# A fused attention and gMLP block on one core: first loads from two queues, all h tiles transposed by DMA, no centred keys, part of the 1/sigma work on GpSimd, and early idle products on a constant

## The chip, the cores and the metric

The kernel runs on one core of one Trainium2 chip. A core has TensorE (PE, matrix products), VectorE (DVE), ScalarE (ACT), GpSimd (POOL) and SyncE (SP, which here only issues transfers); 16 DMA engines move the data. The metric is the time of one execution on the device in microseconds (us). The kernel before was timed three times: 246.90, 246.95 and 247.34 us, median 246.95 us.

## The reference

One sequence of 2048 tokens with 512 features in bf16 goes through two residual blocks. `ln` is layernorm over the features without gain or offset.

```
h   = x + A(ln(x))
out = h + B(ln(h))

A(u):  q, k, v = split(u @ wqkv)              # 32 heads of 16 features
       phi(t) = (t + 1 if t > 0 else exp(t)) + 1e-6
       kv  = sum over tokens of phi(k) v^T     # 16 x 16 per head
       z   = sum over tokens of phi(k)
       o   = (phi(q) kv) / (phi(q) . z + 1e-6)
       return o @ wo
B(u):  z   = gelu(u @ w_in)                    # 512 -> 1792
       z1, z2 = halves of z, 896 features each
       g   = w_sp @ ln(z2) + b_sp              # w_sp: 2048 x 2048, mixes the tokens
       return (z1 * g) @ w_out                 # 896 -> 512
```

## The kernel before

All of the data stays in SBUF. The 2048 tokens are 16 tiles of 128 tokens, and four groups of four tiles. Every operation is recorded by `op(engine, cost, ...)` with what it reads and writes; a list `ORDER` (lines 15 to 52) then says in which order the operations go to the five instruction queues, and a list `SLOT` which PSUM bank or buffer each temporary tile gets. Each engine works through its queue strictly in that order, and waits by semaphores are added where an operand comes from another engine. So the order of the work on each engine is written out, and an instruction whose operand is late holds up all that stand behind it on its engine.

The stages, with the lines that matter here:

1. Loads (lines 503 to 513). SP issues x tiles 0, 1, 2-3, then the key weights `wk`, then x tiles 4-5, 6-7, 8-11, 12-15 and the query weights `wq`, in this order. The weights `wv`, `wo`, `w_in` come later from POOL (lines 709 to 711), once the last transpose of x has landed.
2. Idle products (lines 548 to 552). While the first tiles are on their way, PE runs 14 products of 128x512 on a tile of zeros, which VectorE clears first (line 516). They compute nothing that is used.
3. Layernorm of x (lines 619 to 640). For each tile, `stats` (line 557) and `aggr` (line 561) on VectorE give mean and variance; Ln and Exp on ScalarE (`rstd_act`, lines 571 and 573) give 1/sigma, from tile 4 on for two tiles at a time; `normalise` (line 583) on VectorE writes the normalised tile. Then it is transposed (`transposed`, line 598): tiles 2 to 5 by four PE products against an identity (line 612) and a ScalarE copy out of PSUM (line 615), the others by a DMA transpose that SP issues (line 604). Tiles 0 and 1 have a second path (`CENTRED`): the tile less its mean, not yet divided by sigma (line 633), is transposed by PE, and their keys are made from it; 1/sigma comes in as the scale of ScalarE's Exp and Relu on the product (line 649).
4. Keys and queries. `kv_proj` makes the keys of a pair of tiles (line 673), `phi` applies exp (line 652), for some pairs also Relu (line 654), and finishes on VectorE: with a min (line 655) and an add (line 658) where Relu was taken by ScalarE, and with the min and one longer instruction from PSUM (line 661) where it wasn't. PE then adds up x^T phi(k) over all tiles (line 705), from which kv follows later without making v. `q_proj` (line 687) makes the queries transposed, a group of four tiles at a time, and so needs all four transposed tiles of that group.
5. The denominators (`den`: lines 787 to 818), and `h`: the products of line 837, the residual add of line 842, stats and aggr of h, 1/sigma on POOL (`rstd_pool`, lines 576 and 578, and `minus`, lines 593 and 594), `normalise_act` on ScalarE (line 589), and the transpose of the normalised h tile: tiles 0 to 3 by PE and a ScalarE copy, tiles 4 to 15 by DMA. ORDER takes group 1 first, then 2 and 3, and group 0 last.
6. The gMLP: z2 by token tiles (line 869), its gelu (line 874), stats and normalisation; z1 transposed by feature blocks (line 900), which needs a whole group of h; the mixing products with the DMA-transposed `w_sp` (line 939, transposes issued on line 915); the gate on VectorE (946, 948); the last projection (957), residual (963) and store (965).

SP's queue is one row: the loads, the 12 DMA transposes of x, the 16 transposes of the first quarter of w_sp, the 12 of h, the other 48 of w_sp, the stores. POOL's queue holds, among the 1/sigma work of h, the load of `b_sp` (line 927), whose buffer lies over that of phi's temporaries and is free only when the last of these has been read (line 814).

Of the kernel before, what the change touches and what calls it, by code (L numbers as in the profile page):

```python
# [10 lines left out]
P = 128  # L11
# [4 lines left out]
    28, 9, 16, 0, 23, 15, 24, 29, 1, 14, 25, 30, 2, 10, 31, 17, 3, 20, 32, 18, 4, 33, 12, 19, 5, 34, 13, 43, 26, 6,  # L16
    35, 11, 52, 27, 36, 7, 21, 44, 37, 53, 8, 45, 38, 48, 22, 39, 54, 57, 46, 49, 68, 58, 40, 55, 47, 41, 61, 42, 56,
    137, 50, 62, 69, 51, 75, 63, 138, 70, 64, 77, 71, 65, 139, 76, 78, 66, 72, 79, 89, 67, 73, 80, 97, 74, 149, 140,
    81, 84, 82, 141, 119, 150, 83, 99, 85, 142, 120, 158, 87, 86, 143, 151, 88, 159, 144, 59, 145, 152, 160, 60, 90,
    147, 153, 146, 91, 148, 92, 100, 161, 154, 93, 156, 95, 94, 155, 127, 157, 162, 219, 96, 220, 98, 128, 109, 101,  # L20
    102, 117, 164, 221, 166, 103, 110, 167, 118, 104, 129, 222, 107, 168, 121, 130, 223, 122, 131, 251, 108, 224,
    169, 125, 252, 123, 111, 105, 170, 163, 106, 165, 112, 253, 171, 257, 115, 113, 254, 172, 258, 114, 132, 174,
    255, 259, 135, 177, 116, 133, 256, 260, 178, 124, 173, 261, 179, 186, 262, 126, 175, 180, 176, 181, 187, 134,
    183, 188, 185, 136, 182, 189, 196, 605, 197, 190, 191, 205, 606, 198, 215, 184, 206, 607, 199, 217, 200, 193,
    207, 192, 608, 276, 216, 208, 277, 609, 209, 270, 210, 278, 610, 271, 279, 194, 611, 272, 201, 280, 218, 281,
    273, 612, 203, 231, 211, 274, 613, 275, 213, 232, 234, 195, 233, 202, 614, 204, 212, 214, 615, 263, 235, 295,
    264, 616, 282, 265, 236, 283, 617, 266, 284, 237, 296, 267, 269, 618, 238, 239, 297, 241, 242, 268, 289, 298,
    619, 243, 290, 240, 299, 620, 285, 300, 291, 342, 288, 292, 343, 286, 357, 293, 344, 358, 294, 225, 347, 301,
    287, 226, 302, 359, 387, 303, 227, 345, 304, 388, 360, 305, 346, 348, 307, 349, 228, 351, 372, 350, 306, 373,
    352, 361, 362, 353, 402, 229, 355, 354, 363, 230, 364, 417, 366, 374, 365, 418, 356, 367, 389, 368, 403, 370,  # L30
    369, 244, 377, 245, 390, 371, 246, 464, 465, 404, 470, 466, 419, 471, 480, 375, 472, 422, 247, 481, 378, 248,
    250, 577, 482, 467, 578, 423, 249, 574, 579, 405, 621, 575, 391, 483, 376, 325, 392, 381, 576, 379, 484, 380,
    308, 420, 382, 485, 309, 421, 393, 406, 383, 424, 407, 396, 394, 486, 385, 473, 426, 384, 395, 474, 425, 487,
    310, 397, 386, 326, 427, 398, 475, 488, 313, 580, 399, 327, 400, 571, 430, 401, 311, 572, 581, 489, 428, 502,
    330, 573, 503, 328, 496, 312, 490, 504, 331, 314, 408, 512, 491, 315, 329, 468, 317, 316, 505, 497, 409, 332,
    469, 506, 318, 513, 476, 498, 410, 507, 591, 477, 322, 333, 499, 334, 588, 514, 411, 478, 335, 412, 479, 582,
    492, 592, 500, 493, 413, 515, 518, 494, 414, 495, 589, 516, 501, 519, 517, 508, 590, 509, 323, 583, 520, 510,
    585, 511, 415, 521, 528, 324, 416, 522, 584, 523, 438, 524, 525, 336, 429, 439, 527, 337, 586, 440, 526, 431,
    319, 529, 441, 622, 587, 534, 442, 443, 320, 530, 544, 623, 321, 604, 531, 545, 338, 532, 624, 432, 339, 533,
    546, 448, 625, 547, 449, 548, 433, 626, 450, 549, 550, 434, 451, 627, 551, 452, 599, 435, 552, 628, 453, 436,  # L40
    600, 553, 340, 554, 629, 593, 601, 437, 555, 444, 602, 556, 341, 445, 630, 557, 454, 603, 446, 559, 631, 569,
    447, 558, 455, 570, 632, 535, 456, 563, 536, 633, 457, 564, 458, 537, 634, 596, 565, 459, 538, 460, 597, 461,
    539, 635, 540, 560, 541, 598, 463, 462, 636, 561, 543, 542, 670, 562, 637, 671, 672, 673, 638, 674, 675, 566,
    639, 676, 677, 640, 567, 678, 680, 679, 568, 641, 642, 643, 683, 681, 644, 682, 645, 686, 646, 684, 685, 647,
    648, 689, 687, 649, 688, 650, 651, 692, 690, 652, 691, 653, 695, 654, 693, 694, 655, 656, 594, 696, 657, 698,
    697, 595, 658, 659, 701, 660, 699, 700, 661, 662, 704, 702, 663, 703, 664, 665, 707, 705, 706, 666, 667, 710,
# [9 lines left out]
    2, 3, 0, 0, 1, 6, 2, 3, 4, 3, 2, 2, 1, 0, 6, 4, 2, 2, 6, 0, 4, 0, 2, 0, 6, 6, 6, 4, 0, 0, 4, 6, 2, 6, 4, 6, 0, 6,  # L56
    2, 0, 0, 4, 0, 2, 2, 7, 0, 6, 0, 7, 1, 6, 2, 7, 3, 6, 0, 7, 1, 6, 2, 4, 3, 5, 0, 4, 1, 5, 2, 4, 0, 5, 1, 4, 2, 5,
    3, 4, 3, 5, 0, 4, 1, 5, 2, 4, 3, 5, 0, 4, 1, 5, 0, 4, 1, 5, 2, 4, 3, 5, 2, 4, 3, 5, 0, 4, 1, 5, 2, 4, 3, 5, 0, 4,
    1, 5, 2, 4, 3, 5, 0, 4, 1, 5, 2, 4, 3, 5, 0, 4, 1, 5, 2, 4, 3, 2, 0,
]  # L60


# [972 lines left out]
```

## Time and profile before

| what | us |
|---|---|
| median of three runs | 246.95 |
| the profiled execution | 247.78 |
| span of its profile, first to last instruction | 246.0 |
| PE busy | 240.4 |
| VectorE busy | 135.6 |
| ScalarE busy | 89.2 |
| POOL busy | 26.4 |

The span is 1.8 us shorter than the execution that it comes from: what lies around the first and last instruction is not in it. PE is busy for 98% of the span, in products that overlap: a 128x512 product lasts 379 ns by itself, and in a row one starts every 216 ns (96 products of line 939 in 20.72 us). A wait in this profile is idle time of an engine and is put down to what ended it; as ends of products are modelled, a gap in PE's row of products is up to 0.2 us longer than its wait.

### The profile page before, as it was taken

To read this page: it belongs to the slowest core of one execution; us is meant where nothing else is said; L and a number is where in the kernel's file an instruction comes from. 1 tells how busy PE (TensorE), PEld (TensorE's weight loads), DVE (VectorE), ACT (ScalarE), POOL (GpSimd) and SP (SyncE) were. 2 spreads that over 40 slices of the span, in tenths; PEclk is the share of its full clock that TensorE was granted. 3 is DMA by queue.
4 is the path that set the end of the run, shared out by engine and by line. 5 is a ranking of instruction groups with operands and counts; after the bars stand their busy time and mean duration, and the time that the engine had idled before them with its cause. 6 is when DMAs were issued, how large, how long until landed. Compare 5 with 4: busy or idle time off the path is not lost.

```text
span 246.0 us, 3055 instructions
## 1 busy us (share of the span) xinstructions
PE 240.4 (98%) x1189; PEld 109.6 (45%) x1189; DVE 135.6 (55%) x272; ACT 89.2 (36%) x125; POOL 26.4 (11%) x75
## 2 busy tenths in 40 slices
PE   7898999999999999999999999999999999999995
PEld 3443444344334444554444444444444444444443
DVE  5899654579999987585422331352322523323443
ACT  3766946696697777966410010000000000000000
POOL 6000003000503373302300000000000000000000
PEclk9999999999999999999999999999999999999999
DMA  6913358984142301596344444443000110000022
GB/s 199 331 24 68 64 100 248 351 106 94 21 67 85 81 9 31 109 237 95 87 102 98 103 85 101 97 101 109 0 0 0 43 45 0 0 0 3 0 85 85
DMA packets 54494, 21.30 MB, mean 87 GB/s; under 512 B 48368, under 2 KB 53616, under 8 KB 54480
## 3 DMA queue, kind: packets, MB, share of 16 engines
q1 hardware_dynamic: 53536, 16.79, 30.7%
q0 software_dynamic: 944, 4.33, 5.2%
q8 instruction: 9, 0.15, 0.3%
q14 instruction: 5, 0.04, 0.1%
HBM read 7.47 MB, written 2.10 MB: 39 GB/s over the span
## 4 chain that ended last, share of the span: by engine, by line
PE 83%; DVE 6%; ACT 5%; DMA 3%; POOL 1%; issue 0%
PE ps L939 39%; PE ps L957 10%; PE ps L900 10%; PE ps L869 9%; PE ps L673 4%; PE ps L705 4%; PE ps L687 3%; PE ps L550 2%; DMA xT_pq_z<-pk_xn_z 2%; DMA hT<-xn 2%; PE ps L837 1%; DVE small L557 1%; ACT e L649 1%; DVE xh L842 1%; ACT e L652 1%; DVE e L655 1%
## 5 line engine op out<-in xcount | busy, mean ns | idle before, releaser
L939 PE MATMUL ps<-wsp,pk_xn_z 128*128 128x512 bf16 x336 | 73.5, 379 | 0.0
L946 DVE TENSOR_TENSOR e<-ps,e 128x512 bf16<-128x512 f32 x28 | 19.4, 692 | 69.0 <-PE ps L939 69.0
L939 PEld LDWEIGHTS ps<-wsp,pk_xn_z 128*128 128x128 bf16 x336 | 32.9, 98 | 39.6
L869 PE MATMUL ps<-win,hT 128*128 128x384 bf16 (+1 forms) x128 | 26.2, 353 | 0.2 <-DMA hT<-xn 0.2
L900 PE MATMUL ps<-hT,win 128*128 128x512 bf16 x112 | 26.3, 379 | 0.0
L905 ACT ACTIVATE xT_pq_z<-ps 128x1024 bf16<-128x1024 f32 (+1 forms) x16 | 14.6, 915 | 31.6 <-PE ps L900 31.6
L957 PE MATMUL ps<-wout,xT_pq_z 128*128 128x512 bf16 (+1 forms) x119 | 24.7, 366 | 0.0
L939 PE MATMUL ps<-wqkv_wsp,pk_xn_z 128*128 128x512 bf16 x112 | 24.3, 379 | 0.0
L557 DVE BATCH_NORM_STATS2 small<-xh 128x6 f32<-128x512 bf16 x32 | 20.8, 677 | 2.7 <-DMA xh<-in_A_x_dram 2.7
L878 DVE BATCH_NORM_STATS2 small<-pk_xn_z 128x6 f32<-128x512 bf16 (+1 forms) x32 | 18.5, 610 | 4.9 <-ACT pk_xn_z L874 4.9
L652 ACT ACTIVATE e<-ps 128x1024 bf16<-128x1024 f32 x15 | 15.4, 1028 | 6.8 <-PE ps L673 5.6
L869 PEld LDWEIGHTS ps<-win,hT 128*128 128x128 bf16 x128 | 12.2, 98 | 12.6 <-DVE xh L842 0.6
L963 DVE TENSOR_TENSOR e<-ps,xh 128x512 bf16<-128x512 f32 (+1 forms) x17 | 11.2, 660 | 11.3 <-PE ps L957 11.2
L957 PEld LDWEIGHTS ps<-wout,xT_pq_z 128*128 128x128 bf16 x119 | 11.7, 98 | 12.8
L939 PEld LDWEIGHTS ps<-wqkv_wsp,pk_xn_z 128*128 128x128 bf16 x112 | 10.9, 98 | 13.2
L900 PEld LDWEIGHTS ps<-hT,win 128*128 128x128 bf16 x112 | 10.8, 98 | 12.1
L705 PE MATMUL ps<-pk_xn_z 128*128 128x512 bf16 x64 | 15.8, 379 | 0.0
L874 ACT ACTIVATE pk_xn_z<-ps 128x896 bf16<-128x896 f32 x16 | 14.3, 914 | 3.1 <-PE ps L869 3.0
L687 PE MATMUL ps<-xT_pq_z,wqkv_wsp 128*128 128x512 bf16 x64 | 15.3, 380 | 0.0
L673 PE MATMUL ps<-wqkv_wsp,xT_pq_z 128*128 128x512 bf16 x56 | 13.9, 380 | 1.4 <-DMA xT_pq_z<-pk_xn_z 0.8
L837 PE MATMUL ps<-pk_xn_z,xT_pq_z 128*128 128x512 bf16 x64 | 14.8, 379 | 0.2 <-ACT e L812 0.2
L589 ACT ACTIVATE xn<-xh,small 128x512 bf16<-128x512 bf16 x16 | 12.6, 810 | 3.7 <-POOL small L594 3.7
(82 smaller groups left out, 190.6 us busy)
## 6 DMA issues: line engine op xcount, KB each, us to landing
out_dram<-e SPq DMA_DIRECT2D x15, 128.0 KB, 1.7
win<-in_B_w_in_dram POOLq DMA_DIRECT2D x1, 1792.0 KB, 9.1
wqkv_wsp<-in_A_wqkv_dram SPq DMA_DIRECT2D x2, 512.0 KB, 6.1
xh<-in_A_x_dram SPq DMA_DIRECT2D x2, 512.0 KB, 6.6
wout<-in_B_w_out_dram POOLq DMA_DIRECT2D x1, 896.0 KB, 6.6
xh<-in_A_x_dram SPq DMA_DIRECT2D x3, 256.0 KB, 4.9
wsp<-in_B_w_sp_dram SPq DMA_TRANSPOSE x48, 2.9
wqkv_wsp<-in_A_wqkv_dram POOLq DMA_DIRECT2D x1, 512.0 KB, 4.9
```

Source lines behind the costliest of these rows:

```text
L557: op("dve", dve_c(512), lambda e: e.bn_stats(s6.ap(), src.ap()), r=[src], w=[s6])
L652: op("act", act_c(n), lambda e: e.activation(lo.ap(), t(flat).ap(), ACT.Exp), r=[t()], w=[lo])
L673: i = e.matmul(t(bank(ti)).ap(), lhsT=lhs.ap()[:, c, :], rhs=rhs.ap()[:, c, :], start=(c == 0), stop=(c == KD - 1))
L687: r_ = e.matmul(t(bank(i)).ap(), lhsT=lhs.ap()[:, c, :], rhs=rhs.ap()[:, c, :], start=(c == 0), stop=(c == KD - 1))
L705: r = e.matmul(txk[h](bank(i)).ap(), lhsT=xx.ap()[:, c * P:(c + 1) * P], rhs=kk.ap(), start=(n == 0), stop=(n == NT - 1))
L837: i = e.matmul(t(bank(ti)).ap(), lhsT=l.ap()[:, c, :], rhs=mw[c, :].ap(), start=(c == 0), stop=(c == KD - 1))
L869: k = e.matmul(t(bank(i)).ap()[:, 0:b - a], lhsT=l.ap()[:, c, :], rhs=win[c, a:b].ap(), start=(c == 0), stop=(c == KD - 1))
L878: op("dve", dve_c(b - a), lambda e, s6=s6, src=src: e.bn_stats(s6.ap(), src.ap()), r=[src], w=[s6])
L900: k = e.matmul(t(bank(i)).ap(), lhsT=l.ap()[:, c, :], rhs=r_.ap()[:, c, :], start=(c == 0), stop=(c == KD - 1))
L939: k = e.matmul(t(bank(0)).ap(), lhsT=l.ap()[:, s - a, :], rhs=r_.ap()[:, s - a, :], start=(s == 0), stop=(s == NT - 1))
L946: op("dve", dve_c(512), lambda e: e.tensor_tensor(gb().ap(), t(bank(0)).ap(), bsp().ap()[:, tg * GW:(tg + 1) * GW], ALU.add), r=[t(), bsp( ...
L957: k = e.matmul(t(bank(0)).ap()[:, 0:b - a], lhsT=l.ap()[:, fc, :], rhs=wout[fc, a:b].ap(), start=(fc == 0), stop=(fc == KF - 1))
```

## The change

The loads of x tile 1 and of x tiles 2-3 are issued by ScalarE, ahead of its table load; `wk` follows x tile 0 at once in SP's queue. The keys of tiles 0 and 1 are made from the normalised tile as the others are; tiles 0 to 5 are transposed by PE, tiles 6 to 15 by DMA. All 16 tiles of h are transposed by DMA. For tiles 4-5, 6-7, 8-9, 10-11, 12-13 and 14-15 of x, 1/sigma is worked out by POOL (an add and a power) and no longer by ScalarE (Ln and Exp). Relu is taken by ScalarE for key pairs 1, 3, 5 and 7 (before: 0, 3, 5 and 7). The tile of zeros is gone: nine 128x512 idle products and fourteen 128x128 ones read a constant 1.0 that the program always has, with a step of zero. Eleven of the short ones stand right behind the nine, one each between the first three transposes, and the last behind the key product of tile 3.

ORDER and SLOT are new as a whole. What moved in the queues: on PE all four query products of group 0 now stand between key product 4 and the first uses of the keys (line 705); before, two of them stood behind those and two at the end of the h stage; group 0 of h is made first and not last; the z2 tiles go 0 to 8, 10, 13, 11, 14, 15, 12, 9. On VectorE, tile 1's stats come ahead of tile 0's, and tile 0 is normalised behind the stats of tiles 2 and 3. On POOL, `wo` is loaded ahead of `wv` and `w_in`, and `b_sp` is loaded behind the 1/sigma of h tiles 0 to 3. On SP the transposes of h tiles 0 to 3 stand ahead of those of tiles 4 to 15.

```diff
@@ -13,50 +13,50 @@
 
 
 ORDER = [
-    28, 9, 16, 0, 23, 15, 24, 29, 1, 14, 25, 30, 2, 10, 31, 17, 3, 20, 32, 18, 4, 33, 12, 19, 5, 34, 13, 43, 26, 6,
...
+    1, 14, 0, 28, 22, 16, 2, 19, 3, 17, 29, 27, 4, 15, 18, 30, 23, 5, 31, 9, 6, 24, 32, 10, 7, 33, 44, 11, 12, 25, 8,
...
 ]
 SLOT = [
-    0, 1, 2, 3, 6, 7, 2, 4, 0, 4, 2, 0, 1, 6, 2, 6, 1, 0, 1, 6, 2, 0, 0, 6, 1, 0, 0, 0, 2, 2, 1, 6, 6, 4, 0, 6, 2, 1,
...
+    0, 1, 2, 3, 1, 2, 3, 4, 0, 0, 6, 6, 1, 2, 2, 2, 2, 4, 2, 4, 1, 2, 2, 4, 0, 2, 0, 0, 4, 1, 3, 0, 0, 6, 4, 6, 4, 1,
...
 ]
 
 
@@ -373,13 +373,17 @@
     TPG = GW // P
     NP = NT // 2
     assert D == 512 and KD == 4 and NG == 4 and FH == KF * P and 512 < FH <= 1024
-    WARM = 14
+    WARM = 9
+    FILL = 14
     EPS_PHI, EPS_DEN, EPS_LN = 1e-6, 1e-6, 1e-5
     CG = 32
-    X_BY_PE, H_BY_PE = (2, 3, 4, 5), (0, 1, 2, 3)
+    X_BY_PE, H_BY_PE = (0, 1, 2, 3, 4, 5), ()
     Q_RELU = (True, True, True, True)
-    K_RELU = (3, 5, 7)
-    CENTRED = (0, 1)
+    K_RELU = (1, 3, 5, 7)
+    CENTRED = ()
+    R_POOL = (4, 6, 8, 10, 12, 14)
+    COPY_DVE = ()
+    LN1 = [[0], [1], [2], [3], [4, 5], [6, 7], [8, 9], [10, 11], [12, 13], [14, 15]]
     N2_ACT = range(16)
     VIA_ACT = ((0, 0), (1, 0), (2, 0), (3, 0))
 
@@ -410,8 +414,8 @@
     pqT = [View(s_tq, (NG + g_) * GB_, [KD, GW], BF16) for g_ in range(NG)]
     z1T = [View(s_tq, 2 * g_ * GB_, [KF, GW], BF16) for g_ in range(NG)]
     hT = [View(s_hT, g_ * GB_, [KD, GW], BF16) for g_ in range(NG)]
-    xc = View(s_hT, 0, [2, D], BF16)
-    xcT = View(s_hT, 2 * D * 2, [KD, 2 * P], BF16)
+    xc = View(s_hT, 0, [4, D], BF16)
+    xcT = View(s_hT, 4 * D * 2, [KD, 4 * P], BF16)
     pk = View(s_kv, 0, [NT, D], BF16)
     xn1 = View(s_kv, pk_b, [NT, D], BF16)
     gz2 = View(s_kv, 0, [NT, FH], BF16)
@@ -437,7 +441,6 @@
     part = small([CG], BF16)
     eps = small([4], FP32)
     nhalf = small([8], FP32)
-    zeros = small([GW], BF16)
 
     psum = nc.alloc_psum_tensor("ps", [P, 8, 512], FP32)
 
@@ -497,23 +500,25 @@
     BIG = 1000.0
 
     def load_x(eng, a, b, bias=BIG, **kw):
+        more = {2: 50e3}.get(a, 0)
         xl[a] = load(eng, f"x{a}", x[a:b, :], x_dram[a * P:b * P, :].rearrange("(n p) d -> p n d", p=P),
-                     (b - a) * P * D * 2, bias, **kw)
+                     int((b - a) * P * D * 2 + more), bias, **kw)
 
     load_x("sp", 0, 1)
-    load_x("sp", 1, 2)
-    load_x("sp", 2, 4)
-    load("sp", "wk", wqkv[:, D:2 * D], w3[:, :, D:2 * D], D * D * 2)
+    load_x("act", 1, 2)
+    load_x("act", 2, 4)
+    load("sp", "wk", wqkv[:, D:2 * D], w3[:, :, D:2 * D], D * D * 2 + 100000)
     for a in (4, 6):
         load_x("sp", a, a + 2)
     for a in (8, 12):
         load_x("sp", a, a + 4)
     load("sp", "wq", wqkv[:, 0:D], w3[:, :, 0:D], D * D * 2)
-    for a, b in zip(g.ops, g.ops[1:]):
-        b.after.append(a)
-
-
-    op("dve", 0.3, lambda e: e.memset(zeros.all().ap(), 0.0), w=[zeros.all()], bias=BIG)
+    for eng in ("sp", "act"):
+        mine = [o for o in g.ops if o.eng == eng]
+        for a, b in zip(mine, mine[1:]):
+            b.after.append(a)
+    first_act = mine
+
     op("pool", 0.25, lambda e: e.memset(ident.all().ap(), 0.0), w=[ident.all()], bias=BIG)
     op("pool", 0.3, lambda e: e.affine_select(ident.all().ap(), ident.all().ap(), pattern=[[-1, P]],
                                               compare_op=ALU.not_equal, fill=1.0, base=0, channel_multiplier=1),
@@ -543,13 +548,18 @@
             sel3, sel3, pattern=[[-(CG * DH // P), P // DH], [0, DH]], compare_op=ALU.not_equal, fill=1.0,
             base=-CG * c, channel_multiplier=1), r=[sel.all()], w=[sel.all()], bias=BIG)
 
-    op("act", 1.3, lambda e: e.preload_act_table_set("natural_log_exp_and_others"), bias=BIG - 1)
+    op("act", 1.3, lambda e: e.preload_act_table_set("natural_log_exp_and_others"), bias=BIG - 1, after=first_act)
 
     idle = Tile(PS)
+    warm = []
+
+    def keep_busy(n, cost, after):
+        row = nc.const_aps.tensor(1.0, (P, n), BF16)
+        return op("pe", cost, lambda e: e.matmul(idle(bank(0)).ap()[:, 0:n], lhsT=row[:, 0:P], rhs=row, start=True,
+                                                 stop=True), w=[idle()], bias=BIG, after=after)
+
     for i in range(WARM):
-        op("pe", 2 * MM if i < 8 else MM, lambda e: e.matmul(
-            idle(bank(0)).ap(), lhsT=zeros[0:P].ap(), rhs=zeros.all().ap(), start=True, stop=True),
-           r=[zeros.all()], w=[idle()], bias=BIG if i < 9 else -BIG)
+        warm = [keep_busy(512, 2 * MM + 0.4 * (i == 0), warm)]
 
 
     def stats(src, st):
@@ -611,12 +621,15 @@
             for c in range(KD):
                 i = e.transpose(o[:, c * P:(c + 1) * P], src().ap()[:, c * P:(c + 1) * P], ident.all().ap())
             return i
-        op("pe", 4 * MS, tr, r=[src(), ident.all()], w=[t()], bias=bias)
+        op("pe", 4 * MS, tr, r=[src(), ident.all()], w=[t()], bias=bias, after=warm)
+        if n in COPY_DVE and dst is not hT:
+            op("dve", dve_c(512), lambda e: e.tensor_copy(
+                d.ap(), t(as_bf).ap()[:, 0:D].rearrange("p (c t) -> p c t", c=KD)), r=[t()], w=[d], bias=bias)
+            return
         op("act", act_c(512), lambda e: e.activation(
             d.ap(), t(as_bf).ap()[:, 0:D].rearrange("p (c t) -> p c t", c=KD), ACT.Copy), r=[t()], w=[d], bias=bias)
 
 
-    LN1 = [[0], [1], [2], [3], [4, 5], [6, 7], [8, 9], [10, 11], [12, 13], [14, 15]]
     last_lnexp = []
     first = {}
     rs_of = {}
@@ -633,7 +646,10 @@
                 op("dve", dve_c(512, 4) + 0.1, lambda e, n=n, m=m, c=c: e.tensor_scalar(
                     c.ap(), x[n, :].ap(), m.ap(), None, op0=ALU.subtract), r=[x[n, :], m], w=[c])
                 transposed(n, lambda c=c: c, xcT, True)
-        rstd_act(st_x[grp[0]:grp[-1] + 1, 7], rs.all())
+        if grp[0] in R_POOL:
+            rstd_pool(st_x[grp[0]:grp[-1] + 1, 7], rs.all(), len(grp))
+        else:
+            rstd_act(st_x[grp[0]:grp[-1] + 1, 7], rs.all())
         for i, n in enumerate(grp):
             d = xn1[n, :]
             normalise(d, x[n, :], Row(st_x, n), 6, rs[i:i + 1])
@@ -661,6 +677,8 @@
             op("dve", dve_c(n), lambda e: e.scalar_tensor_tensor(
                 flat(dst.ap()), t(flat).ap(), 1.0 + EPS_PHI, lo.ap(), op0=ALU.add, op1=ALU.max), r=[t(), lo], w=[dst])
 
+    k_pe = []
+
     def kv_proj(p, col):
         t = Tile(PS, 2)
         for ti in range(2):
@@ -673,7 +691,7 @@
                     i = e.matmul(t(bank(ti)).ap(), lhsT=lhs.ap()[:, c, :], rhs=rhs.ap()[:, c, :], start=(c == 0),
                                  stop=(c == KD - 1))
                 return i
-            op("pe", 4 * MM, mm, r=[lhs, rhs], w=[t()])
+            k_pe.append(op("pe", 4 * MM, mm, r=[lhs, rhs], w=[t()]))
         return t
 
     def q_proj(gq, f):
@@ -976,6 +994,10 @@
     for n in range((NG - 1) * TPG, NT):
         project(n, [(0, D)] if n < NT - 1 else [(0, D // 2), (D // 2, D)])
 
+    g.late, g.bias = False, 0.0
+    for i in range(FILL):
+        keep_busy(P, 0.06, [] if i < FILL - 1 else [k_pe[3]])
+
     g.schedule()
 
     with nc.Block() as block:
```

80 rows, old and new, of tables (ORDER, SLOT) are left out of this document.

## The prediction

> **What bounds the kernel now.** I read the page's engine rows first, then PE's waits, then the chain that ended last, then stretches of one microsecond over the start.
>
> ```profile
> span 246.0 us, 3055 instructions
> PE 240.4 (98%) x1189; PEld 109.6 (45%) x1189; DVE 135.6 (55%) x272; ACT 89.2 (36%) x125; POOL 26.4 (11%) x75
> PE   7898999999999999999999999999999999999995
> ```
>
> PE is the bound: only its first four slices of 6.15 us are not full. So two things can move the end: fewer products on PE, or fewer holes in its queue.
>
> ```profile
> PE ps L550 <- DVE small L516: 1.2, 1, 1.2
> PE ps L673 <- DMA xT_pq_z<-pk_xn_z: 0.8, 1, 0.8
> PE ps L673 <- ACT xT_pq_z L615: 0.6, 1, 0.6
> PE ps L869 <- DMA hT<-xn: 0.2, 1, 0.2
> PE ps L837 <- ACT e L812: 0.2, 1, 0.2
> ```
>
> These are all of PE's waits. The last two stand for holes of 0.40 and 0.34 us between products (71.98 to 72.38, 63.00 to 63.34), 0.74 us together.
>
> ```profile
> 1.24 4.88 PE ps L550 x11
> 6.12 0.43 PE ps L612 x4
> ...
> 6.87 0.22 PE ps L612 x4
> ...
> 7.52 1.74 PE ps L673 x8
> ...
> 17.61 0.60 DVE small L557
> 18.21 0.34 DVE pk_xn_z L661
> 18.55 4.15 DMA xT_pq_z<-pk_xn_z
> ...
> 22.75 1.04 PE ps L673 x4
> ...
> 67.66 0.84 ACT xn L589 x2
> 68.50 3.74 DMA hT<-xn
> 72.24 0.14 issue
> 72.38 1.02 PE ps L869 x4
> ```
>
> To be seen: products start slow (a 512-wide idle product takes 0.43 us, four transposing ones 0.43) and run at double pace after 6.5 us, though the granted clock reads 1.00 in every row; a DMA transpose takes about 3.7 us from its normalised tile to PE; and the last wait before PE runs full is key product 7 at 22.75, for x tile 7.
>
> ```profile
> 2.00:3.00 1.00, 1.00 (x4) 0.38 (x3) 0.08 (x1) 0.07 (x1) 0.97 (x7) 1.00 0.82 245
> 3.00:4.00 1.00, 1.00 (x4) 0.38 (x3) 1.00 (x2) 0.00 (x0) 1.00 (x5) 1.00 0.68 231
> 5.00:6.00 1.00, 1.00 (x4) 0.39 (x3) 1.00 (x2) 0.10 (x1) 0.00 (x0) 1.00 1.05 369
> ```
>
> The DMA engines (last two columns: share, GB/s) are full from 4 to 12 us, and not from 2 to 4.
>
> **Loads.** Three issues of SP take 1.33 us, 0.44 each; two leave SP's queue, so wk, the later x tiles and wq are issued 0.9 us earlier. They stand ahead of ScalarE's table load (1.28 us from 0.78), which ends at 2.9 and not 2.06; ScalarE's first Ln ran at 4.38, so that is covered. What lands when? Tiles 4-5 made VectorE wait until 7.62. At best they come 0.9 earlier; but the engines are full, and x2-3 now shares them with wk, so at worst 0.3 later. I take no change. In the Trainium skill, "DMA: Bandwidth & Descriptors", section "Issuing engines are not separate DMA queues", a second issuing engine saves only the sequencer's time, since all queues share the same 16 engines; by that the loads would be worth nothing from tile 4 on, which is the value taken, while the 245 and 231 GB/s between 2 and 4 us leave room for more.
>
> **Idle products.** The clearing of zeros goes, so PE starts with the other engines at 0.8 and not 1.24. Nine slow products (9 x 0.43) and eleven short ones (0.43/4 each) end at 5.9. Cost nothing: the first transpose isn't ready before 6.1. The one short product behind key 3 costs 0.06.
>
> **Start of the keys.** VectorE now: stats of tiles 1 and 0 from 2.95, 0.60 each; two aggr, 0.1 each; stats 2 and 3; aggr 2; normalise 0 (0.32) ends at 6.0, tile 2 at 6.7. Two centrings (0.31 each) are gone. ScalarE's copy of tile 0 (0.5 to 0.6) follows at 6.55, key 0 at about 7.2 (before: 7.36); if x2-3 lands 0.6 later, 7.8, and key 2 still isn't held up, for it waits for tile 3's transpose. Tile 3 is normalised behind stats 5 and 4 (7.6 + 1.2 + 0.2 + 0.3 = 9.3), so PE waits 0.45 there, and 0.45 again for tile 4 (10.8). Tile 5 is ready at 11.25. From key 3 at 11.57 PE has 3 keys, 4 queries of group 0 (0.863 each), 8 half products of line 705 (0.432) and no wait that I find: wq lands at 4.80 + 7.9 = 12.7 at the latest and the first query stands at 13.3. So PE is at key 6 at 21.1.
>
> **What is late next: x tiles 6 and 7.** VectorE works from 7.6 without a break: stats x10 (5, 4, 7, 9, 6, 13, 10, 15, 12 and the rest) at 0.60 make up most of 10.1 us until tile 6 is normalised, at 17.7 (before: 17.3 for tile 6, 17.6 for 7). Swapping key pair 0 and 1 between the add (0.64) and the long instruction (1.17) leaves VectorE's sum as it was, four of each. Before, tile 6 was in use 3.6 us after its issue at the latest and tile 7 4.15 after 18.55. So key 6 at 21.4 to 21.95, key 7 at 22.7 to 23.2, where it was 22.75. But by then PE has done two more queries and one half product less: 1.73 - 0.43 = 1.30. Gain 1.1 us, between 0.8 and 1.35. The two DMA transposes that go (x tiles 0 and 1) were not ahead of a late one: SP stood waiting for normalised tiles.
>
> **1/sigma on POOL.** Six Ln/Exp pairs (0.29 + 0.20) leave ScalarE; POOL gets 12 instructions (0.24 and 0.73), 1.1 us a pair with the hops, in a queue idle until 36.7. Nearest to the path is tiles 4-5: aggr at 9.0, power done at 10.15, normalise 4 at 10.5. Nothing, up to 0.3 if POOL's constants are late. The loads of wo, wv, w_in stand behind these and behind the last transpose of x; w_in has till 67.
>
> **h tiles by DMA.** Sixteen PE products go: the chain has 0.22 for each four (at 95.00), so 0.88 us off a full PE. Four copies of 0.6 leave ScalarE, which has idle time. SP gets four issues of 1.2 us behind the first w_sp quarter (34.87 to 60); the h tiles come at 63. The w_sp quarters behind them end some 5 us later; the second quarter began at 100.8, takes 16 x 1.5 and is used at 147, so covered.
>
> **Holes in the h stage.** Group 0 comes first. With the rows above: the copy of mw (1.03, behind an exp and a Relu) holds the first product of line 837 by 0.4. Tile 0's norm ends at 63.2, its transpose lands by 67.0, PE is there at 67.3: none. Tile 2 lands at 70.7, PE is there at 70.3: 0.4. The product of group 3 waits for its division, behind stats z0, which waits for the gelu and its 1.28 us table load: 0.5. The load of b_sp waits on the same division and blocks POOL until 75.5, and h tiles 4-5 need POOL at 76: none. The last z2 tile, 9, needs gelu, stats, POOL, normalise, 5.2 us by the rows at 114 to 120, against six products of 0.863: 0.1. Sum 1.4 against 0.74 before: 0.66 lost; between 0.6 gained (no hole) and 1.8 lost (each hole 0.3 longer, four of them).
>
> **Sum.** -1.1 - 0.88 + 0.66 = -1.3 us: span 246.0 to 244.7, the profiled execution 247.78 to 246.5. The median of the runs is 0.83 below that execution: 246.95 - 1.3 = 245.65, say 245.6. Own range from the bounds: 1.35 + 0.88 + 0.6 = 2.8 gained (244.1), 0.8 + 0.88 - 1.8 = 0.1 lost (247.0).
>
> **Rivals.** First, slower: the transposes of h group 0 become PE's wait. Speaks for it: one DMA transpose in the trace took 6.7 us to land, the others 2.5; PE's order has nothing to put in between tile 0 and tile 3. If tiles 0 to 3 come 4.2 us later, PE loses that less the 0.3 of slack: 3.9, so 249.5; half as much late gives 247.4. It decides from 1.8 us late on, where gain and 0.5 more are gone. Against: the 6.7 us one ran beside the loads at 350 GB/s, and around 61 to 72 us the traffic is 21 to 67. Chance 0.20, time about 248.
>
> Second: the clock. PE has a hole from 5.9 to 6.1 before the first transpose, and short products ahead of it. If the fast pace needs the 5.2 us of unbroken work that it took before (1.24 to 6.5), it comes at 11.3: keys 0 and 1 take 1.73 each, key 3 starts 1.2 later, the waits for tiles 6 and 7 hide 0.4 to 0.7 of that. 246.1 to 246.8, middle 246.4. Against: the hole is small. The Trainium skill, "TensorE: Matmul & The Clock Gate", Part 1, has free-running windows of about 3.4 us and full clock after one busy window; 5.2 us until the fast pace fits a window from about 3.1 to 6.5, and a hole at its end might or might not spoil it, which no row here tells. Chance 0.12, half of it within 0.2%.
>
> Third: the two queues fill the engines from 2 us on. 350 GB/s there and not 240 is 0.22 MB, 0.6 us for x4-5; VectorE's run and tiles 6 and 7 come that much earlier, and the h stage has no hole more than before (0.66): 1.3 + 1.3, so 244.3. Chance 0.13.
>
> **Numbers.** The forecast has 0.55. What can be told from no change is 0.2%, 0.5 us. Faster by more: 0.48 + 0.13 + 0.06 = 0.67; within: 0.05 of the forecast's own range, 0.06 of the clock, 0.02 of the first rival, 0.13; slower: 0.18 of the first rival and 0.02 of the forecast's slow end, 0.20. The range goes from the third rival to the first: 244.0 to 248.2.
>
> **To look for.** In the changed profile: idle products from 0.8; first key product at 7.2; a wait at key 6 or 7 by DMA xT, key 7 near 23.0 with four queries before it; no row of line 612 from xn; waits of line 869 on DMA hT of 0.5 or less; mixing starts about 1.3 us earlier. Wrong if PE's first waits sum to more than 2.5 us or line 869 waits more than 2 us for hT.

## The result and the profile after

The changed kernel takes 248.24 us (median of 12 runs, 247.85 to 251.32). The kernel before, run beside it, takes 247.59 us (12 runs, 246.9 to 248.27). The ratio is 1.0043, with a 95% interval of 1.0022 to 1.0064: slower by 0.4%, where 0.5% faster was forecast. By the medians it is 0.65 us, or 0.3%. Ratios leave out executions that took over 1.5% longer than the fastest of the same kernel. The profiled execution of the changed kernel took 248.01 us, with a span of 246.2 us.

The page of the changed kernel: its span, the engines, and the slices of PE and of its granted clock.

```profile
span 246.2 us, 3018 instructions
PE 238.5 (97%) x1160; PEld 109.8 (45%) x1182; DVE 134.9 (55%) x269; ACT 84.7 (34%) x107; POOL 33.1 (13%) x87
PE   7799999999998999999999999999999999999995
PEclk9799999999999999999999999999999999999999
```

PE is busy for 1.9 us less than before (240.4), and yet the span is 0.2 us longer. About 1.1 of the 1.9, by estimate, is an artefact of the profile: 22 of the 1182 products (PE x1160 beside PEld x1182) have no record, and each leaves some 0.05 us of idle time in the chain. The clock's second slice (6.15 to 12.3 us) reads 7. The same row of the kernel before has full clock in every slice:

```profile
PEclk9999999999999999999999999999999999999999
```

PE's waits in the changed kernel (total, times, longest, in us):

```profile
PE ps L622 <- DVE pk_xn_z L593: 2.3, 1, 2.3
PE ps L558 <- PEq L1042: 0.8, 1, 0.8
PE ps L855 <- DVE xT_pq_z L832: 0.7, 1, 0.7
PE ps L705 <- issue: 0.2, 1, 0.2
```

The wait at key 7 for a DMA transpose is gone, and so are the two holes of 0.40 and 0.34 us in the h stage. In their place stand one wait of 2.3 us for the first normalised x tile, and one of 0.7 for the division of group 3. The chain that ended last (start, length) says where the 2.3 come from:

```profile
1.23 5.01 DMA xh<-in_A_x_dram
6.24 0.02 issue
6.26 1.29 DVE small L567 x2
7.55 0.08 DVE small L571
7.63 0.31 DVE pk_xn_z L593
7.94 0.05 issue
7.99 0.40 PE ps L622 x4
...
9.35 3.12 PE ps L691 x8
```

The load of x tiles 2-3, now on ScalarE's queue, is issued at 1.23 and lands 5.01 us later, at 6.24. In the kernel before, SP issued it at about 1.7 and it took 2.9 us, so it landed at about 4.6: the load now goes out half a microsecond earlier and lands 1.6 us later. Nor does `wk` gain: issued 0.93 us earlier, at 1.24, it takes 5.2 us where it took 4.2, and lands at about 6.4 as before. VectorE takes its work in order: stats of tiles 2 and 3 stand ahead of the normalisation of tile 0, whose 1/sigma was ready at 5.89 (ScalarE's Exp, 5.56 + 0.33). So tile 0 waits for the bytes of tiles 2-3, and PE for tile 0: the first transpose is at 7.99, and the idle products end at 5.69.

The last line is the second half of the story. Keys 0 and 1 take 3.12 us. The kernel before needed 1.74. Stretches of one microsecond (PE, PEld, DVE, ACT and POOL busy, granted clock, DMA share, GB/s):

```profile
7.00:8.00 1.00, 0.01 (x1) 0.02 (x2) 1.00 (x5) 0.30 (x2) 0.00 (x0) 1.00 1.11 352
8.00:9.00 1.00, 1.00 (x13) 0.86 (x14) 1.00 (x4) 0.96 (x4) 0.00 (x0) 0.80 1.10 349
9.00:10.00 1.00, 1.00 (x7) 0.45 (x5) 1.00 (x5) 1.00 (x4) 0.00 (x0) 0.50 1.10 348
11.00:12.00 1.00, 1.00 (x4) 0.31 (x3) 1.00 (x4) 0.00 (x0) 0.23 (x1) 0.50 0.66 206
12.00:13.00 1.00, 1.00 (x9) 0.57 (x8) 1.00 (x3) 0.51 (x1) 0.00 (x0) 1.00 0.00 0
```

PE works without a break from 8.0 on, and the granted clock is 0.50 from about 8.6 to 12.0. Then it is 1.00 for good. After the hole, PE pays a second time.

Where the time stands: key 7 starts at 24.98, and at 22.75 before. PE has done 1.30 us more by then (two queries more, one half product less), so the start loses 2.23 - 1.30 = 0.93 us. The h transposes give 0.88 back, and the holes of the h stage are 0.7 against 0.74. 0.93 - 0.88 leaves 0.05; the spans differ by 0.2, and the rest is not accounted for.

### The profile page after: what moved, and what is told of

Its sections match the earlier page's. It is cut to its first block, busy times and chain, and to the rows that moved or that the text cites. A ratio compares the mean times of both kernels' runs of the same rounds, so it can differ in the third digit from the quotient of the medians.

```text
span 246.2 us, 3018 instructions
## 1 busy us (share of the span) xinstructions
PE 238.5 (97%) x1160; PEld 109.8 (45%) x1182; DVE 134.9 (55%) x269; ACT 84.7 (34%) x107; POOL 33.1 (13%) x87
## 4 chain that ended last, share of the span: by engine, by line
PE 85%; DVE 6%; ACT 5%; DMA 2%; POOL 1%; issue 1%; ACTq 0%
PE ps L957 39%; PE ps L975 10%; PE ps L918 9%; PE ps L887 8%; PE ps L691 6%; PE ps L723 6%; PE ps L705 4%; DMA xh<-in_A_x_dram 2%; DVE small L567 2%; PE ps L855 1%; ACT e L668 1%; DVE xh L860 1%; DVE xT_pq_z L835 1%; ACT e L670 1%; DVE xT_pq_z L832 1%
## 5 line engine op out<-in xcount | busy, mean ns | idle before, releaser
L668 ACT ACTIVATE e<-ps 128x1024 bf16<-128x1024 f32 x16 | 16.4, 1026 | 11.2 <-PE ps L691 7.0
L981 DVE TENSOR_TENSOR e<-ps,xh 128x512 bf16<-128x512 f32 (+1 forms) x17 | 11.2, 660 | 11.3 <-PE ps L975 10.9
L588 POOL TENSOR_TENSOR small<-small 128x2 f32<-128x2 f32 x22 | 16.8, 766 | 1.3
L691 PE MATMUL ps<-wqkv_wsp,xT_pq_z 128*128 128x512 bf16 x63 | 16.8, 406 | 0.1
L957 PEld LDWEIGHTS ps<-wqkv_wsp,pk_xn_z 128*128 128x128 bf16 x112 | 10.9, 98 | 13.2
L918 PEld LDWEIGHTS ps<-hT,win 128*128 128x128 bf16 x112 | 10.9, 98 | 12.4
```

The costliest lines, as they stand in the source:

```text
L668: op("act", act_c(n), lambda e: e.activation(lo.ap(), t(flat).ap(), ACT.Exp), r=[t()], w=[lo])
L691: i = e.matmul(t(bank(ti)).ap(), lhsT=lhs.ap()[:, c, :], rhs=rhs.ap()[:, c, :], start=(c == 0), stop=(c == KD - 1))
L918: k = e.matmul(t(bank(i)).ap(), lhsT=l.ap()[:, c, :], rhs=r_.ap()[:, c, :], start=(c == 0), stop=(c == KD - 1))
L957: k = e.matmul(t(bank(0)).ap(), lhsT=l.ap()[:, s - a, :], rhs=r_.ap()[:, s - a, :], start=(s == 0), stop=(s == NT - 1))
```

## The experiments

Theory 1: the two loads on ScalarE's queue arrive late, because they are in flight beside what SP loads. Theory 2: the order in VectorE's queue is at fault (tile 0's normalisation behind stats 2 and 3), and the loads matter little. Both may hold. A separate question is what the loss of pace costs. Ratios are to the kernel before, run on the same chip at the same time. The experiments ran on three chips, where the median of the kernel before lay between 247.38 and 247.78 us, so a difference of 0.2 or 0.3 us between medians of two experiments says little.

**Loads back on SP.** The changed kernel, with its x loads issued by SP in the old sequence.

```
-    load_x("act", 1, 2)
-    load_x("act", 2, 4)
+    load_x("sp", 1, 2)
+    load_x("sp", 2, 4)
 ORDER:
-    1, 14, 0, 28, 22, 16, 2, 19, 3, 17, 29, 27, 4, 15, 18, 30, 23, 5, 31, 9, 6, 24, 32, 10, 7, 33, 44, 11, 12, 25, 8,
+    14, 28, 22, 16, 19, 17, 29, 27, 0, 1, 2, 3, 4, 15, 18, 30, 23, 5, 31, 9, 6, 24, 32, 10, 7, 33, 44, 11, 12, 25, 8,
```

> The changed kernel, its first four loads issued by SP again in the old order (x0, x1, x2-3, wk); all else as changed. Theory 1 (shared engines: x0, x1 and x2-3 landed late because they were in flight beside wk): stats of the first tiles start at 2.95 and not 3.70, stats of tile 2 by 4.9 and not 6.26, tile 0 is normalised at 6.0, the first transpose runs at about 6.1 and not 7.99, PE's hole ahead of it shrinks from 2.3 us to 0.4, and the time falls by about 2.3 us against the changed kernel, to about 246 (before: 247.6). Rival A (the landing is set by the 16 engines, whichever queue issues): all of this as in the changed kernel, 248.2. Rival B (even a hole of 0.4 us drops TensorE's pace): start early, but keys 0 and 1 take 3.1 us and not 1.73, about 247.2.

Measured: 245.34 us (245.25 to 245.69), ratio 0.9902 (0.9875 to 0.9928). From the timeline of this run:

```profile
4.82 1.25 DVE L566 BATCH_NORM_STATS2 small<-xh 128x6 f32<-128x512 bf16 x2
6.51 0.40 PE L621 MATMUL ps<-small,pk_xn_z 128*128 128x128 bf16 x4 [1.52 <-DVE pk_xn_z L592]
7.60 1.90 PE L690 MATMUL ps<-wqkv_wsp,xT_pq_z 128*128 128x512 bf16 x8
```

Stats of tiles 2-3 run at 4.82 with no wait, against 6.26. The first transpose comes 1.48 us earlier, after a hole of 1.52, and the keys run at full pace (1.90 in this view, where the changed kernel has 3.31). Two lines of the change, the loads, turn 1% faster into 0.4% slower: 2.90 us between the medians. Two expected figures were missed. The first stats run at 3.40 and not at 2.95, since VectorE's queue begins with tile 1, which lands after tile 0. The hole is 1.52 and not 0.4, since the first transpose comes 0.4 later than expected and the idle products end at 4.99 and not at 5.69, although nothing about them was changed.

**Filling the hole.** The changed kernel, with 24 more short idle products ahead of the first transpose. It loads as the changed kernel does and adds work that nobody needs.

```
-    FILL = 14
+    FILL = 38
```

> The changed kernel with 24 more short idle products (128x128) behind the eleven, which fill PE's hole from 5.7 to 8.0; nothing else. Theory 3 (the hole makes TensorE fall back to half pace): the first transpose still starts at about 8.0, but keys 0 and 1 take 1.73 us and not 3.12, the granted clock reads 1.00 throughout; about 1.2 us less than the changed kernel, 247.0. Rival (the pace has another cause, or VectorE holds the later keys anyway): the same time, 248.2.

Measured: 246.78 us (246.31 to 247.5), ratio 0.9967 (0.9951 to 0.9983). Timeline:

```profile
8.53 0.40 PE L622 MATMUL ps<-small,pk_xn_z 128*128 128x128 bf16 x4 [0.71 <-DVE pk_xn_z L593]
9.62 1.90 PE L691 MATMUL ps<-wqkv_wsp,xT_pq_z 128*128 128x512 bf16 x8
```

The first transpose is even 0.54 later than in the changed kernel, and the kernel is 1.46 us faster, because the clock stays up. The clocks of all executions say the same: none of these 12 has a mean granted clock below 0.999, and 10 of the changed kernel's 12 have one of 0.993 or 0.986. A stretch of 3.4 us at half clock lowers the mean of a span of 246 us to 0.993. So the 2.90 us of the first experiment fall into roughly 1.46 for the pace and 1.44 for the lateness itself; roughly, because in this profile the stats of tiles 2-3 start 0.55 later (6.81) than in the changed kernel's, with the same loads.

**Tile 0's normalisation ahead.** The changed kernel, with the loads left on the two queues, normalisations 0 and 1 put ahead of stats 2 and 3, and what follows from them moved along.

```
 ORDER:
-    34, 37, 20, 35, 26, 45, 36, 38, 21, 51, 46, 13, 39, 47, 58, 40, 52, 41, 53, 59, 48, 796, 797, 798, 799, 800, 801,
+    34, 37, 20, 35, 26, 45, 36, 38, 21, 46, 39, 47, 40, 41, 48, 796, 797, 798, 799, 800, 801, 802, 803, 804, 805, 806,
...
```

> The changed kernel with another order at the start only: VectorE normalises tiles 0 and 1 before the stats of tiles 2 and 3, ScalarE copies their transposes before the Ln of tile 2, PE makes keys 0 and 1 before it transposes tile 2. Loads as in the changed kernel. Theory 2 (tile 0 was ready, its normalisation stood in VectorE's queue behind stats that waited for the load of x2-3): the first transpose at about 6.3 and not 8.0, the hole 0.6 us, key 0 at 7.2 to 7.5, about 1.5 us less than the changed kernel, 246.7. Rival (wk lands late too, or tile 3 is what key 2 waits for): key 0 earlier but key 2 as late, the gain under 0.5 us.

Measured: 246.71 us (246.54 to 246.93), ratio 0.9955 (0.9935 to 0.9976). Timeline:

```profile
6.06 0.40 PE L621 MATMUL ps<-small,pk_xn_z 128*128 128x128 bf16 x4 [1.03 <-DVE pk_xn_z L592]
10.86 0.40 PE L621 MATMUL ps<-small,pk_xn_z 128*128 128x128 bf16 x4 [1.31 <-DVE pk_xn_z L592]
```

Tile 0 now comes at 6.06, earlier than in the first experiment, and the clock stays up. But the tiles behind it are still late, and PE waits 1.31 for the next of them. Both theories hold in part: without its place behind stats 2 and 3, tile 0 makes no long hole (1.53 us gained, about what filling the hole gained, and again no execution of the 12 has a clock below 0.999), and the late loads still cost about 1.4 us further on.

**The two queues alone.** The kernel before, with its x1 and x2-3 loads issued by ScalarE ahead of its table load.

```
-    load_x("sp", 1, 2)
-    load_x("sp", 2, 4)
+    load_x("act", 1, 2)
+    load_x("act", 2, 4)
...
-    for a, b in zip(g.ops, g.ops[1:]):
-        b.after.append(a)
+    for eng in ("sp", "act"):
+        mine = [o for o in g.ops if o.eng == eng]
+        for a, b in zip(mine, mine[1:]):
+            b.after.append(a)
```

> The kernel before with the loads of x1 and x2-3 issued by ScalarE ahead of its table load, as in the changed kernel; all else as before. Theory 1: x0 and x1 land at 3.7 and x2-3 at 6.3 here too. But in the order of before, idle products cover tile 0 until 5.9 and tile 2 is normalised behind stats 4 and 5, which waited until 7.62: so at most 0.2 us slower, 247.6 to 247.8. Rival (late landing goes through to the end as it is): 1.0 to 1.4 us slower, about 248.8.

Measured: 248.59 us (247.71 to 252.34), ratio 1.0024 (1.0003 to 1.0044). Timeline:

```profile
5.91 0.63 PE L613 MATMUL ps<-small,hT 128*128 128x128 bf16 x4
6.11 1.29 DVE L558 BATCH_NORM_STATS2 small<-xh 128x6 f32<-128x512 bf16 x2 [0.63 <-DMA xh<-in_A_x_dram]
```

The loads are nearly as late as in the changed kernel (6.11 against 6.26, and 3.46 against 3.70 for the first two tiles). They cost 0.6 us by the ratio and 0.9 by the medians (247.69 for the kernel before): more than the 0.2 expected, a little less than the rival's 1.0 to 1.4, and well below the 2.90 that they cost the changed kernel. So the expectation failed as a number, and the cost is not a property of the loads alone. In the profile the first transpose is at 5.91 as before, because the centred tile that it takes is made ahead of stats 2 and 3 and needs no 1/sigma. The centred keys would thus be the cover that the change removes, but this is read from one trace, of the fastest of the 12 executions: three others have a granted clock of 0.993 (249.09 to 252.34 us), and no run put the centred keys back into the changed kernel.

**Only x1 on ScalarE.** The changed kernel, with x2-3 back on SP ahead of wk.

```
-    load_x("act", 2, 4)
+    load_x("sp", 2, 4)
```

> The changed kernel with x1 still issued by ScalarE, but x2-3 by SP ahead of wk. Theory 1, narrowed: what hurts is x2-3 in flight beside wk, not x1 beside x0. Then the stats of tile 2 start by 5.0 and not 6.26, the first transpose by 6.6, and the time is within 0.5 us of the kernel with all loads on SP (245.3). Rival (any load on a second queue delays the first ones): stats of tile 2 at 6 or later, 247 to 248.

Measured: 246.12 us (245.23 to 246.86), ratio 0.9928 (0.9904 to 0.9951). Stats 2-3 run at 5.07 with no wait. A wait of 0.4 for wk appears, and tiles 4-5 come late, in a profile that is of the slowest of the four executions (246.86):

```profile
8.95 1.29 DVE L566 BATCH_NORM_STATS2 small<-xh 128x6 f32<-128x512 bf16 x2 [1.53 <-DMA xh<-in_A_x_dram]
```

The stats and the first transpose (6.76) came about as expected; the time is 0.8 us above 245.3, where 0.5 was allowed. Still, 2.12 of the 2.90 us come back with x2-3 ahead of wk: issued by SP at 1.70, they land 3.0 us later. Against all loads on SP (0.9902) x1 alone costs some 0.3%, and the two intervals overlap. Over all profiles x2-3 takes 4.8 to 5.5 us from ScalarE's queue and 2.8 to 3.6 from SP's. No run put x2-3 on ScalarE's queue with wk behind them, so for x2-3 the queue and the neighbour are not told apart. For x0 they are: SP issues it first and at the same time in every version, and it takes 2.4 to 2.7 us where ScalarE issues x1 beside it, and 2.0 to 2.2 where SP issues x1 behind it.

**The price of the h transposes, at group 0.** From here on the experiments build on the first one. This one adds 16 products of 128 columns ahead of the z2 products of tiles 0 to 3: as many as the change removed.

```
-            def mm(e, t=t, i=i, a=a, b=b, l=l):
+            def mm(e, t=t, i=i, a=a, b=b, l=l, n=n):
+                for c in range(KD if i == 0 and n < 4 else 0):
+                    e.matmul(t(bank(i)).ap()[:, c * P:(c + 1) * P], lhsT=l.ap()[:, c, :], rhs=win[c, a:a + P].ap(),
+                             start=True, stop=True)
```

> The changed kernel with its loads on SP, and with sixteen more 128-wide products on PE, four ahead of the z2 products of each of h tiles 0 to 3, written to PSUM and overwritten: what the PE transposes of the four h tiles cost PE, without their copies. The step of the prediction (0.88 us off a full PE): 0.9 us more than without them, 246.2. Rival (PE has slack at that place, so the products that went were free): under 0.3 us more, 245.3 to 245.6.

Measured: 245.58 us (245.2 to 246.29), ratio 0.992 (0.9903 to 0.9937): 0.24 more than without them, with intervals that overlap. The timeline of the first experiment has, at the product that waits for the division of group 3,

```profile
74.48 1.04 PE L854 MATMUL ps<-pk_xn_z,xT_pq_z 128*128 128x512 bf16 x4 [0.67 <-DVE xT_pq_z L831]
```

and here the same product has no wait in front:

```profile
74.35 1.04 PE L854 MATMUL ps<-pk_xn_z,xT_pq_z 128*128 128x512 bf16 x4
```

0.88 less 0.67 is 0.21: the added products fell into a hole. This measured the hole, and not the price.

**The price where PE is full.** The same 16 products, ahead of z2 of tiles 11, 12, 14 and 15.

```
+                for c in range(KD if i == 0 and n in (11, 12, 14, 15) else 0):
```

> The changed kernel with its loads on SP and sixteen more 128-wide products, this time four ahead of the z2 products of each of tiles 11, 12, 14 and 15, where no hole follows. If PE is full there: 0.9 us more than without them, 246.2, and then it was the hole of 0.7 us behind tiles 0 to 3 that took up the same products in the run before. Rival (transposing products cost PE less than their 0.22 us a tile): under 0.4 us more.

Measured: 246.36 us (246.17 to 247.92), ratio 0.9947 (0.9927 to 0.9967): 1.02 above the first experiment's median. That is near 0.88; the intervals of the two ratios just touch, so its size is not known closely. Its profiled execution happens to be the slowest of the eight, and its start shows the pace lost, with the loads on SP and a hole that is only 0.27 longer than the first experiment's:

```profile
7.03 0.40 PE L621 MATMUL ps<-small,pk_xn_z 128*128 128x128 bf16 x4 [1.79 <-DVE pk_xn_z L592]
8.19 3.30 PE L690 MATMUL ps<-wqkv_wsp,xT_pq_z 128*128 128x512 bf16 x8
```

In the same execution PE waits for a transposed h tile, which no other profile of the loads on SP shows; the wait for the division is gone from it:

```profile
PE ps L889 <- DMA hT<-xn: 0.9, 1, 0.9
```

**All of 1/sigma on ScalarE.** The first experiment without POOL's part.

```
-    R_POOL = (4, 6, 8, 10, 12, 14)
+    R_POOL = ()
```

> The changed kernel with its loads on SP, 1/sigma of all x tiles by ScalarE's Ln and Exp at the same places of the order. The step of the prediction (moving it to POOL is worth nothing, up to 0.3 either way): 245.0 to 245.6. Rival (POOL's 1.1 us a pair holds the normalisation of tiles 4 and 5, so ScalarE is better): 0.3 to 0.6 us faster. Other rival (ScalarE was late with Ln and Exp behind its long instructions): 0.5 us slower or more.

Measured: 245.59 us (245.53 to 246.29), ratio 0.9925 (0.9906 to 0.9944). The difference, 0.25 us of the medians, is inside the intervals: POOL's part is worth nothing that can be told.

**Both moves together.** The first experiment, with tile 0's stats ahead of tile 1's, tiles 0 and 1 normalised ahead of the stats of tile 3, keys 2 and 3 pulled forward, and the stats of z0 (operation 419) behind the division of group 3.

```
 ORDER:
-    34, 37, 20, 35, 26, 45, 36, 38, 21, 51, 46, 13, 39, 47, 58, 40, 52, 41, 53, 59, 48, 796, 797, 798, 799, 800, 801,
+    8, 34, 20, 35, 26, 38, 45, 36, 21, 51, 39, 40, 46, 47, 41, 48, 796, 797, 798, 799, 800, 801, 802, 803, 804, 805,
...
```

> The changed kernel with its loads on SP and three moves in the order: tiles 0 and 1 are normalised ahead of the stats of tile 3, key 2 is made ahead of tile 3's transpose and key 3 ahead of those of tiles 4 and 5; the stats of z2 tile 0 stand behind the division of group 3. If PE is the bound from key 3 on and the 0.7 us hole in the products of line 854 came from those stats: key 3 is done 0.5 us earlier and the hole is gone, together 0.5 to 1.2 us less than with the loads alone, 244.1 to 244.8. Rival (VectorE's run behind the load of x4-5 sets keys 4 to 7 whatever stands ahead of them): 0 to 0.5 us, 244.8 to 245.3.

Measured: 246.49 us (246.31 to 247.35), ratio 0.9957 (0.9941 to 0.9973): worse than the loads alone (0.9902) and than both ranges expected. The first transpose came at 5.95, but the tiles behind it were now held up by ScalarE's copies:

```profile
PE ps L690 <- ACT xT_pq_z L628: 2.6, 4, 0.9
```

An earlier first tile was worth nothing here, because those that followed came one by one. The hole at the division was gone.

**The division's move alone.** The first experiment, with 419 moved behind 294.

```
 ORDER:
-    417, 325, 422, 373, 418, 423, 419, 432, 424, 329, 292, 361, 433, 293, 295, 553, 434, 294, 438, 554, 331, 605, 386,
+    417, 325, 422, 373, 418, 423, 432, 424, 329, 292, 361, 433, 293, 295, 553, 434, 294, 419, 438, 554, 331, 605, 386,
```

> The changed kernel with its loads on SP; the stats of the first half of z2 tile 0 stand behind the division of group 3 in VectorE's queue, nothing else moved. The hole of 0.7 us ahead of a product of line 854 is what VectorE loses by waiting for the gelu there: hole gone, 0.5 to 0.7 us less than with the loads alone, 244.7. Rival (the transposes of h tiles 4 and 5, behind the same VectorE run, become PE's wait instead): no gain, 245.3.

Measured: 244.84 us (244.48 to 246.04), ratio 0.9898 (0.9872 to 0.9924). PE's waits in the profiled execution are down to the start's:

```profile
PE ps L621 <- DVE pk_xn_z L592: 1.4, 2, 1.2
PE ps L557 <- PEq L1041: 0.8, 1, 0.8
```

The span is 242.8 (243.6 without the move), so the 0.7 hole came off the end. The ratios (0.9898, 0.9902) don't tell the two apart, because two of the six executions took 246.04 and 245.84. The first of them has a granted clock of 0.993, as the changed kernel has; the second has 1.000 and stays unexplained.

**Tile 0's stats before tile 1's.** The version just shown, in the other order of the first two stats.

```
 ORDER:
-    14, 28, 22, 16, 19, 17, 29, 27, 0, 1, 2, 3, 4, 15, 18, 30, 23, 5, 31, 9, 6, 24, 32, 10, 7, 33, 44, 11, 12, 25, 8,
+    14, 28, 22, 16, 19, 17, 29, 27, 0, 1, 2, 3, 4, 15, 18, 30, 23, 5, 31, 9, 6, 24, 32, 10, 7, 33, 37, 44, 11, 12, 25,
...
```

> As the run with the z2 stats moved, and VectorE takes the stats of x tile 0 ahead of tile 1's (x0 lands 0.4 us before x1 when both are on SP). If the first tile's stats set the start: first transpose 0.3 to 0.4 us earlier; but tiles 4 and 5 still land at 7.4, so 0 to 0.3 us less, 244.4 to 244.8. Rival (the start is bound by x2-3, whose stats come next): no difference.

Operation 37 is tile 0's stats, 44 tile 1's. Measured: 244.91 us (244.58 to 246.48), ratio 0.9903 (0.9869 to 0.9936): no difference, although the first stats start at 2.93 (3.33 in the version just shown) and the first transpose at 6.21 (6.43).

**A shorter hole at the start.** The version with the division's move, and 8 more short idle products.

```
-    FILL = 14
+    FILL = 22
```

> The run with the loads on SP and the z2 stats moved, and eight more short idle products behind the eleven (0.45 to 0.86 us), so that the hole of 1.5 us ahead of the first transpose is about 0.8 us. If that hole is what makes some executions of it slow (one of six had a granted clock of 0.993 and took 1.2 us more): no execution below 0.999, all within 0.5 us of each other, median 244.6. Rival (the spread has another cause): the same spread, 244.5 to 246.0.

Measured: 244.67 us (244.42 to 244.91, six executions), ratio 0.9879 (0.9855 to 0.9902), span 242.7. No execution has a granted clock below 0.999. Timeline:

```profile
0.83 5.27 PE L557 MATMUL ps<-const-bfloat16-1.0 128*128 128x512 bf16 x28 [0.83 <-PEq L1041]
6.48 0.40 PE L621 MATMUL ps<-small,pk_xn_z 128*128 128x128 bf16 x4 [0.38 <-DVE pk_xn_z L592]
```

The idle products leave 0.38 us of hole and don't delay the first transpose (6.43 in the version without them). This is the best version: 1.2% faster than the kernel before and 3.6 us below the changed kernel. The profiled span is only 0.1 shorter than without the 8 products, and the two ratios overlap; that the shorter hole is what kept every execution below 245 is likely, but six executions of each don't show it.

## Why the prediction was wrong

- **Loads ("I take no change").** This is the step that failed. It asked what the two queues do to tiles 4-5, and took the stats of x0 and x1 from 2.95 as before. They ran at 3.70 (3.40 with all loads on SP), and those of x2-3 at 6.26 (4.82). Of the 3.40, 0.47 is the order and not the queues: 2.95 is when tile 0 can start, and VectorE now begins with tile 1 (2.93 with tile 0 first). The step did say that x2-3 shares the engines with wk, and allowed 0.3 late for tile 4-5 and 0.6 for x2-3; it was 1.4. Its evidence, the unused DMA rate between 2 and 4 us, was real, but the second queue did not use it: 223 and 191 GB/s in these two microseconds, 245 and 231 before. And a rate does not say which load is served: x2-3 landed 1.6 us later. The Trainium skill, "DMA: Bandwidth & Descriptors", "Issuing engines are not separate DMA queues", says that DMAs of all issuing engines interleave on the same 16 engines. The runs agree: with wk (SP) in flight beside it, x2-3 (ScalarE) is used at least 1.44 us later than when it is ahead of wk in SP's queue, where VectorE found it landed.
- **Start of the keys (key 0 at 7.2, or 7.8).** It was at 9.14 to 9.35. The step named VectorE's order correctly, stats 2 and 3 ahead of normalise 0, and then took from it that a late x2-3 costs little. With the loads on SP, key 0 was at 7.60, within what the step gave. The queue order made a load that isn't needed for tile 0 decide when tile 0 comes.
- **Idle products ("cost nothing").** They cost nothing, but they end at 5.69 and did not reach the first transpose. The forecast had a hole of 0.2 there, and it was 2.3. With the 0.8 at the start, PE's first waits sum to 3.1 us, above the 2.5 that the forecast named as a sign of being wrong.
- **Second rival, the clock (chance 0.12).** What it feared happened: keys 0 and 1 ran at half pace, until 12.0 where it said 11.3. "Against: the hole is small" was wrong, since it rested on the loads. Its condition, 5.2 us of unbroken work before the fast pace, is not what the trace shows: the first transpose and the short product behind it still run at full pace (0.40 and 0.22 us), and half clock then lasts 3.4 us. Its price, 1.2 for key 3 and 0.5 to 1.2 at the end, compares with 1.46 measured by filling the hole.
- **Third rival, fuller engines from 2 us on (chance 0.13).** It did not occur: 223 and 191 GB/s where it had 350.
- **x tiles 6 and 7 (gain 1.1).** With the loads on SP, key 7 starts at 22.34 without a wait, with the same 1.30 of extra products in front: 1.71 gained. The wait forecast there did not occur in either version. The estimate of VectorE's run to tile 6 was too long (17.7, and 17.1 with the loads on SP), and tile 7's transposed tile was in use 3.50 us after its issue (18.84), where the forecast took up to 4.15.
- **h tiles by DMA (0.88).** Supported: 16 such products cost 1.02 where PE is full. The first rival, transposes late at group 0, did not occur in the changed kernel: no wait of PE on a transposed h tile is left in its profile. It is not ruled out in every execution, since one experiment's profile has such a wait, of 0.9 us.
- **Holes in the h stage (1.4 against 0.74).** Of the four, only one occurred: the product that waits for the division of group 3, 0.7 where 0.5 was forecast. It went away when the stats of z0 were put behind the division, as the step had named the cause. The copy of mw, tile 2 and the last z2 tile (0.9 together) cost nothing. So 0.66 of loss didn't come.
- **1/sigma on POOL (nothing).** Right.

Without the failed step, the other steps of the forecast were too cautious: with the loads on SP the kernel takes 245.34, a gain of 1.0% where 0.5% was forecast. The sign was decided by the loads and by what they did to the clock.

What stays open: whether a hole drops the pace is not settled by its length (below). Two of the changed kernel's 12 executions read a granted clock of 1.000 and still took 248.86 and 249.04; no run tells why.

## What to carry to other kernels

Here a second issuing queue added no DMA rate: it let a large load that can wait (wk, 512 KB) run beside a small one that can't (x2-3, 256 KB), and neither of the two came earlier. Keep the loads in the order of need on one queue, and before moving one, look at what stands behind it in each in-order engine: here a tile that had already landed waited for one that had not. When work is removed from the start of a kernel, ask what its presence was covering, and keep PE busy up to its first real product.

## What the runs showed of the hardware

The pace after a hole early in the kernel was not foreseen. Holes of PE between the idle products and the first transpose, and the pace of the keys behind them, in the profiled executions:

| hole, us | loads of x1, x2-3 | keys 0 and 1, us | granted clock behind it |
|---|---|---|---|
| 0.21 (tile 0's stats first) | SP | 1.90 | 1.00 |
| 0.28 (both moves) | SP | 1.90 | 1.00 |
| 0.38 (8 more idle products) | SP | 1.69 (seven of eight recorded) | 1.00 |
| 0.67 (1/sigma on ScalarE) | SP | 1.90 | 1.00 |
| 0.71 (24 more) | ScalarE | 1.90 | 1.00 |
| 0.94 (16 products at group 0) | SP | 1.90 | 1.00 |
| 1.03 (tile 0 ahead) | ScalarE | 1.90 | 1.00 |
| 1.20 (division's move) | SP | 1.90 | 1.00 |
| 1.52 (loads on SP) | SP | 1.90 | 1.00 |
| 1.78 (x1 on ScalarE) | both | 1.89 | 1.00 |
| 1.79 (16 products later) | SP | 3.30 | 0.50 from about 7.6 to 11.0 |
| 2.30 (the change) | ScalarE | 3.31 | 0.50 from about 8.6 to 12.0 |

Two holes of 1.78 and 1.79 us went different ways, and with tile 0 ahead a second one of 1.31 us, at 9.5 to 10.9, left the clock at 1.00 too, so length isn't all that decides; that it depends on when the hole falls would fit, but was not tested. The hole itself is not fixed by the kernel: the same 20 idle products ended between 4.98 and 6.00 us in ten profiles. So counts over all executions say more than single profiles. A granted clock below 0.999 stands in 10 of the changed kernel's 12 executions; in 2 of the 44 executions of the seven versions with all loads on SP and 20 idle products; and in none of the 30 with 24 more idle products, 8 more, or tile 0 ahead. A hole ahead of the first transpose is not the only way to it: 3 of the 12 executions of the kernel before with two queues have it too, and no trace shows where.

In both profiles with a drop the clock falls some 0.6 us after PE has started again (at 7.99 and 7.03), stays at 0.50 for 3.4 us with PE busy throughout, and returns. Half of 3.4 us is 1.7 us of PE's work; 1.46 us is what filling the hole gave back. The Trainium skill, "TensorE: Matmul & The Clock Gate", Part 1, has free-running windows of about 3.4 us. The length of the drop agrees with one window. The Trainium skill, "TensorE: Matmul & The Clock Gate", section "Why this matters for your kernels", warns of idle gaps above some 3 us. Here 1.79 and 2.30 us were enough, and the measurement decides.
